# One decode step of attention beside an MLP: row 35 of w2 in other pieces, the MLP's bias loaded once, two rounds of V to an accumulator, the last V ahead of w2's row 14

## The chip, the core and the metric

One Trainium2 chip, of which the program uses one core. TensorE (PE, with PEld for its weight loads), VectorE (DVE), ScalarE (ACT), GpSimd (POOL) and SyncE (SP) run side by side; the core's 16 DMA engines bring the data from HBM. The metric is the device time of one execution in microseconds (us), as the median of several runs.

## What is computed

All arrays are float32. x is 2 x 576, the caches are 2 x 32 x 4096 x 128 (134 MB each), wq 576 x 4096, wo 4096 x 576, w1 576 x 4608, w2 4608 x 576.

```
x = A_x
g = sigmoid((x * gate_w).sum(-1))
q = x @ wq                         # 2 x 32 heads x 128
s = q . k_cache * 128**-0.5        # 2 x 32 x 4096
a = softmax(s) @ v_cache @ wo      # 2 x 576
h = gelu(x @ B_w1 + B_b1)          # 2 x 4608
b = h @ B_w2 + B_b2
out = g * a + (1 - g) * b
```

## The kernel before

**Memory.** One tile, `ring`, holds three slots of 64 KB in each of the 128 partitions. SP issues nearly all loads, in one fixed order: wq and w1, then K and V of 16 rounds (k0, v0, k1, v1, ...; each 8.39 MB, one slot, 64 KB to a partition), then three last pieces: rows 0 to 27 of w2; rows 28 to 35 of w2 with the first 16 rows of wo; the other 16 rows of wo. A load is issued when the slot that it goes to is free: after K of a round was reduced to scores (L518), or after TensorE has read V (L544). The transfers use eight completion semaphores in turn (DMAHW0 to DMAHW7 below), so a transfer also waits until the one eight before it has landed. ACT issues the small loads (x, the gate, the biases).

**A round (i = 0 to 15) is four heads of one batch entry.** DVE multiplies K by q in place (L508, `mul`) and sums over the 128 columns (L513, L514, `red`); POOL adds halves of a part of it first (L512). `max_p` (L518) takes each partition's largest score. `max_t` (L523) puts all partitions' maxima on each partition with a TensorE matmul, and `max_n` (L527) takes the maximum of each head, negated. ACT takes exp (L533, `softmax`) into the tile `p`. In the next round TensorE multiplies `p` with V (L544, `av`: 32 matmuls, each recorded as two, since float32 runs as two passes), DVE keeps the wanted diagonal blocks (L556, `keep`), and a matmul with `pick` adds them to the accumulator `oall` (L562, `combine`).

**Around the rounds.** Before them q (`proj` with wq) and the hidden layer of the MLP (`proj` with w1, then bias and gelu into `hg`) are made. After them come the products of `hg` with the rows of w2 (`mlp_out`, L369, into `acc`), the normalisation of `oall` (`norm_sum`, `norm_t`, `o_turn`), and the products with the rows of wo: rows 0 to FOLD - 1 into `acc` (`wo_out`, L369), the others into `res` (`last_out`, L459), to which `acc`, copied by ACT (L448), is folded (L469). The order of TensorE's work there is written out by hand.

**Row 35 of w2.** "Row r" is, for each partition p, the r-th of the 36 rows of w2 that p holds; row 35 is thus 128 places of 576 numbers. In the kernel before, the first 288 columns of it come with rows 28 to 34, in place; the other 288 columns come in four transfers, each over four partitions with eight places each (`wx`, L155), and are multiplied in `mlp_x` with a copy of `hg` spread to the same 16 partitions (`hx`).

Of the kernel before, what the change touches and what calls it, by code (L numbers as in the profile page):

```python
# [19 lines left out]
def kernel(  # L20
# [50 lines left out]
    FOLD = 23  # L71
# [11 lines left out]
    qp = ctx.enter_context(tc.tile_pool(name="qp", bufs=2))  # L83
# [51 lines left out]
    XE, XC = 4, 4  # L135
    XP = XE * XC
    XS = P // XP
    srcx2 = w2.rearrange("(e c s r) n -> c r e s n", e=XE, c=XC, s=XS)[:, NF - 1, :, :, DS:]

    def length(w, a, z):  # L140
        return XS * DS if w == "wx" else (z - a) * D - (DS if (w, z) == ("w2", NF) else 0)

    def load_last(m):
# [5 lines left out]
        for w, a, z in LAST[m]:  # L149
            if w == "wx":  # L150
                xt = t[:XP, o:o + XS * DS]
                rows[w] = xt.rearrange("p (s n) -> p s n", s=XS)
                o += XS * DS
                for c in range(XC):
                    nc.sync.dma_start(xt[c::XC].rearrange("e (s n) -> e s n", s=XS), srcx2[c])  # L155
                continue
            if (w, z) == ("w2", NF):
                nc.sync.dma_start(t[:, o:o + length(w, a, z)], srcs[w][:, a * D:z * D - DS])
                for r in range(a, z):
                    rows[w, r] = t[:, o + (r - a) * D:o + min((r - a + 1) * D, length(w, a, z))]  # L160
                o += length(w, a, z)
# [53 lines left out]
    def load_b1(b, ends):  # L215
        to, src = b1r.rearrange("(g q) n -> g q n", g=NG)[:, b], b1.rearrange("(g n) -> g n", g=NG)
        for u, v in zip(ends, ends[1:]):
            nc.scalar.dma_start(to[:, u:v], src[:, u:v])  # L218


    load_b1(0, (0, F4))
# [11 lines left out]
    idsc = cp.tile([P, P], F32, name="idsc")  # L233
    nc.scalar.mul(idsc, ident, SCALE)

# [6 lines left out]
    for j in range(NPB):  # L242
        t = cp.tile([P, NT * EB + 32 - EB], F32, name=f"p{j}")
# [6 lines left out]
    sel = ident.rearrange("p (j c) -> p j c", j=4)[:, :, :EB].rearrange("p j (e r) -> p j e r", e=E)  # L250
    selr = cp.tile([P, RB], F32, name="selr")
    nc.vector.tensor_reduce(selr, sel.rearrange("p j e r -> p r j e"), AX.XY, ALU.add)
    pick = cp.tile([P, 2 * NO - E], F32, name="pick")
    nc.vector.memset(pick, 0.0)
    nc.vector.tensor_reduce(pick[:, NO - E:NO], sel.rearrange("p j e r -> p e j r"), AX.XY, ALU.add)
# [61 lines left out]
    load_b1(1, (0, 232, 464, 696, 928, F4))  # L317
# [14 lines left out]
    nc.scalar.copy(qall, qps2)  # L332
# [65 lines left out]
    hb = ht[:, :, :B]  # L398
# [13 lines left out]
    for s in range(XS):  # L412
        nc.tensor.matmul(
            hxps[:, s], ident.rearrange("p (q s) -> p s q", s=XS)[:, s], hg[:, NF - 1], start=True, stop=True
# [4 lines left out]
    def mlp_x():  # L419
        for s in range(XS):  # L420
            acc_mm(hx[:, s], rows["wx"][:, s], s, lo=1)

    def mlp_out(lo, hi):
        for r in range(lo, hi):
            acc_mm(hg[:, r], rows["w2", r], r)
# [19 lines left out]
    def last_out():  # L445
# [18 lines left out]
        for r in range(FOLD, 31):  # L464
            for s in range(NC):
                part(r, s)
            if r == FOLD + 3:
# [53 lines left out]
    def max_t(i):  # L521
        mt[i] = ps_sm.tile([P, P], F32, tag="sm", name=f"mt{i}")
        nc.tensor.matmul(mt[i], mx[i].to_broadcast([P, P]), idsc, start=True, stop=True)  # L523

    def max_n(i):
        bias[i] = sp.tile([P, E], F32, tag="bs", name=f"bs{i}")
        nc.vector.tensor_reduce(bias[i], mt[i].rearrange("o (e p) -> o e p", e=E), AX.X, ALU.max, negate=True)  # L527

    def softmax(i):
        p = pt[i % NPB][:, :NT * EB].rearrange("p (t c) -> p t c", c=EB)  # L530
        for e in range(E):
# [3 lines left out]
                bias=bias[i][w, e:e + 1], scale=SCALE, accum_out=rs[w, i * E + e:i * E + e + 1],  # L535
# [3 lines left out]
    def av(i):  # L539
        ps = ps_av.tile([P, 512], F32, tag="av", name=f"av{i}")  # L540
        p = pt[i % NPB]
        for t in range(NT):
# [3 lines left out]
                p[:, EB * t:EB * t + 32],  # L546
                vt[i][:, RB * t:RB * (t + 1)].rearrange("p r d -> p (r d)"),
                start=(t < 4),
                stop=(t >= NT - 4),
            )  # L550
        avs[i] = ps
# [9 lines left out]
    def combine(i):  # L561
        nc.tensor.matmul(  # L562
            oall, pick[:, NO - E - i * E:2 * NO - E - i * E], avs[i].rearrange("p r d -> p (r d)"),
            start=(i == 0), stop=(i == N - 1), skip_group_check=True,
# [19 lines left out]
    for i in range(N):  # L584
        k = i - 1
        if 0 <= k:
            max_n(k)
# [12 lines left out]
        if 0 <= k:  # L600
            keep(k)
# [51 lines left out]
```

## Time and the profile before

| | before |
|---|---|
| time, median of 3 runs (lowest to highest) | 721.52 us (721.48 to 721.54) |
| span of the profiled execution | 719.8 us |
| DMA queue of SP, share of 16 engines' time in that span | 99.2% |
| read from HBM | 308.59 MB |
| busy: DVE, PE, POOL, ACT | 516.8, 237.2, 143.8, 38.3 us |
| PE instructions recorded | 1695 matmuls and as many weight loads |

The span runs from the first to the last instruction of one profiled execution. Its own run's time is not listed; the median is 1.7 us above the span, which is what lies around it. A busy share is an average over stages with different limits, so it is read stage by stage.

### The profile page before, as it was taken

What the parts mean: (1) busy time and instruction counts of PE and PEld (TensorE: products, weight loads), DVE (VectorE), ACT (ScalarE), POOL (GpSimd) and SP (SyncE); (2) the same over time, 40 slices, a digit from 0 to 9 for tenths busy, and PEclk for the clock granted to TensorE, in tenths of its full rate; (3) what the DMA queues carried; (4) which work ended last, traced back from release to release, by engine and by line L of the source; (5) the groups of instructions that cost most, each with busy time, mean ns of one, the idle gap of its engine ahead of it and who ended that gap; (6) DMA issues with size and microseconds to landing.
All of it is one profiled execution on the core that took longest, in us unless ns stands there. A gap on an engine that the chain in (4) does not pass through costs nothing.

```text
span 719.8 us, 3981 instructions
## 1 busy us (share of the span) xinstructions
PE 237.2 (33%) x1695; PEld 72.1 (10%) x1695; DVE 516.8 (72%) x146; ACT 38.3 (5%) x143; POOL 143.8 (20%) x31
## 2 busy tenths in 40 slices
PE   0682022230516060504142140506060503224198
PEld 0330000010101010101010010101010101001033
DVE  0104969789695969596969879696969596978900
ACT  0010010100001010101010100101010101010000
POOL 1000130404050403022040404040503113040400
PEclk9986557575757565755757575757575665757589
DMA  9999999999999999999999999999999999999997
GB/s 409 412 443 431 433 441 419 455 416 448 426 444 427 426 438 430 437 430 441 434 433 433 437 427 437 426 437 434 441 430 444 427 437 422 433 441 431 418 425 307
DMA packets 7277, 308.84 MB, mean 429 GB/s; under 512 B 830, under 2 KB 1362, under 8 KB 1628
## 3 DMA queue, kind: packets, MB, share of 16 engines
q1 hardware_dynamic: 7204, 308.55, 99.2%
q8 instruction: 13, 0.21, 0.1%
q10 hardware_dynamic: 56, 0.05, 0.0%
q14 instruction: 4, 0.03, 0.0%
HBM read 308.59 MB, written 0.00 MB: 429 GB/s over the span
## 4 chain that ended last, share of the span: by engine, by line
DMA 46%; DVE 35%; PE 16%; issue 1%; ACT 1%; ACTq 0%; POOL 0%; DVEq 0%; SPq 0%; POOLq 0%
DMA ring<-in_A_k_cache_dram 41%; DVE ring L508 19%; DVE s L513 10%; PE av L544 8%; DVE s L514 5%; DMA ring<-in_A_wo_dram 3%; DMA ring<-in_gate_w_dram 3%; PE hps L305 2%; PE qps L305 2%; PE oall L562 1%; PE acc L369 1%; PE mt L523 1%; ACT p L533 1%; ACTq L218 0%; DVE m L518 0%
## 5 line engine op out<-in xcount | busy, mean ns | idle before, releaser
L508 DVE TENSOR_TENSOR ring<-ring,q 128x16384 f32<-128x16384 f32 x16 | 275.6, 17225 | 108.9 <-DMA ring<-in_A_k_cache_dram 108.9
L512 POOL TENSOR_TENSOR ring<-ring 128x3968 f32<-128x3968 f32 x16 | 137.0, 8564 | 494.3 <-DVE ring L508 494.3
L513 DVE TENSOR_REDUCE s<-ring 128x66 f32<-128x8448 f32 x16 | 143.2, 8953 | 1.3
L544 PE MATMUL av<-ring,p 128*32 128x512 f32 x1024 | 133.7, 681 | 11.5 <-ACT p L533 6.2
L523 PE MATMUL mt<-idsc,m 128*128 128x128 f32 x32 | 12.6, 498 | 367.5 <-DVE m L518 367.5
L514 DVE TENSOR_REDUCE s<-ring 128x62 f32<-128x3968 f32 x16 | 68.4, 4276 | 0.0
L533 ACT ACTIVATE p<-s,bs 32x128 f32<-32x128 f32 x64 | 25.5, 398 | 487.8 <-DVE bs L527 486.6
L544 PEld LDWEIGHTS av<-ring,p 128*32 128x32 f32 x1024 | 35.6, 124 | 119.3 <-issue 102.4
L523 PEld LDWEIGHTS mt<-idsc,m 128*128 128x128 f32 x32 | 8.0, 310 | 383.2 <-DVE m L518 289.1
L353 PE MATMUL qb<-qm,spread 64*128 64x512 f32 x8 | 8.3, 1138 | 71.2 <-POOL qm L349 71.2
L562 PE MATMUL oall<-avs,pick 128*64 128x512 f32 x32 | 30.6, 1059 | 0.8 <-DVE avs L556 0.8
L556 DVE TENSOR_TENSOR avs<-av,selr 128x512 f32<-128x512 f32 x16 | 10.9, 680 | 16.1 <-PE av L544 16.1
L392 DVE TENSOR_TENSOR ring<-hps,ring 128x384 f32<-128x384 f32 x3 | 1.7, 558 | 27.2 <-PE hps L305 27.0
L263 DVE COPY ring<-ring 3x64 f32<-3x64 f32 x2 | 0.3, 180 | 19.8 <-DMA ring<-in_gate_w_dram 19.8
L349 POOL TENSOR_TENSOR qm<-qall,mine 64x512 f32<-64x512 f32 x4 | 4.1, 1032 | 38.4 <-ACT qall L332 38.4
L533 ACT ACTIVATION_READ_ACCUMULATOR p<-s,bs 32x1 f32 x64 | 11.8, 184 | 0.0
L369 PE MATMUL acc<-ring,hg 128*2 128x288 f32 x142 | 11.6, 456 | 0.0
L305 PE MATMUL hps<-ring 128*32 128x384 f32 x120 | 11.5, 549 | 0.0
L305 PE MATMUL qps<-ring 128*32 128x512 f32 x80 | 11.4, 737 | 0.0
L353 PEld LDWEIGHTS qb<-qm,spread 64*128 64x128 f32 x8 | 2.0, 307 | 74.2 <-POOL qm L349 74.2
L479 DVE COPY ring<-res 2x144 f32<-2x144 f32 x1 | 0.3, 298 | 12.6 <-PE res L483 12.6
L272 PE MATMUL xps<-ident,ring 3*128 3x3 f32 x10 | 1.3, 250 | 23.1 <-DMA ring<-in_gate_w_dram 23.1
(89 smaller groups left out, 75.3 us busy)
## 6 DMA issues: line engine op xcount, KB each, us to landing
ring<-in_B_w_dram SPq DMA_DIRECT2D x2, 4608.0 KB, 34.4
ring<-in_B_w_dram SPq DMA_DIRECT2D x2, 4032.0 KB
ring<-in_A_wo_dram SPq DMA_DIRECT2D x2, 2304.0 KB, 15.0
ring<-in_B_w_dram SPq DMA_DIRECT2D x1, 2160.0 KB
ring<-in_A_wo_dram SPq DMA_DIRECT2D x1, 2016.0 KB
ring<-in_B_w_dram SPq DMA_DIRECT2D x1, 1152.0 KB, 14.7
ring<-in_A_wo_dram SPq DMA_DIRECT2D x1, 1152.0 KB
ring<-in_A_wq_dram SPq DMA_DIRECT2D x1, 1024.0 KB
```

What stands on the lines that cost most here:

```text
L305: nc.tensor.matmul(ps[32 * j:32 * j + 32, :width], lhs, ts[c][:, o:o + width], start=(k == 0), stop=last, skip_group_check=True,)
L353: nc.tensor.matmul(ps, spread, t.rearrange("p u d -> p (u d)"), start=True, stop=True)
L369: nc.tensor.matmul(acc[o:o + m], lhsT, rhs[:, (s - lo) * DS:(s - lo + 1) * DS], start=start, stop=stop, skip_group_check=True)
L508: nc.vector.tensor_mul(kt[i], kt[i], qs[i].unsqueeze(1).to_broadcast([P, R, DH]))
L512: nc.gpsimd.tensor_add(t[:, :, :DH2], t[:, :, :DH2], t[:, :, DH2:])
L513: nc.vector.tensor_reduce(st[i][:, HALVED:], kt[i][:, HALVED:], AX.X, ALU.add)
L514: nc.vector.tensor_reduce(st[i][:, :HALVED], t[:, :, :DH2], AX.X, ALU.add)
L523: nc.tensor.matmul(mt[i], mx[i].to_broadcast([P, P]), idsc, start=True, stop=True)
L533: nc.scalar.activation(p[w, :, e * RB:(e + 1) * RB], st[i][w].rearrange("p (t c) -> p t c", c=RB), AF.Exp, bias=bias[i][w, e:e + 1], scale ...
L544: nc.tensor.matmul(ps[32 * j:32 * j + 32], p[:, EB * t:EB * t + 32], vt[i][:, RB * t:RB * (t + 1)].rearrange("p r d -> p (r d)"), start=(t ...
L556: nc.vector.tensor_mul(t, avs[i].rearrange("p (r d) -> p r d", d=DH), selr.unsqueeze(2).to_broadcast([P, RB, DH]))
L562: nc.tensor.matmul(oall, pick[:, NO - E - i * E:2 * NO - E - i * E], avs[i].rearrange("p r d -> p (r d)"), start=(i == 0), stop=(i == N - ...
```

## The change

It does these things:

- **Row 35 of w2.** Partitions 0 to 31 get their place of row 35, all 576 columns, in place, by a transfer of its own. The other 96 places come in four transfers, each over six partitions with four places each.
- **Bias of the MLP.** b1 was added to each batch row before the transpose, and so was loaded twice (one transfer, and five small ones later). Now it is loaded once, into a third row, and added after the transpose by one more DVE operation.
- **Maximum.** The TensorE matmul L523 and its scaled identity `idsc` are gone: DVE transposes blocks of 32 x 32 instead. The factor 128**-0.5 is applied to q rather than in exp.
- **Accumulating V.** Two rounds go to one accumulator, the one to its upper, the other to its lower half; `keep` and `combine` are done once for two rounds.
- **End.** TensorE's last product with V stands behind row 13 of w2, no longer behind row 23; the rest of w2 is in other places; FOLD is 27 instead of 23.
- TensorE's program has 140 instructions fewer. The q tile has one buffer instead of two.

```diff
-    FOLD = 23
+    FOLD = 27
-    qp = ctx.enter_context(tc.tile_pool(name="qp", bufs=2))
+    qp = ctx.enter_context(tc.tile_pool(name="qp", bufs=1))
...
-    XE, XC = 4, 4
+    XE, XC, XS = 6, 4, 4
     XP = XE * XC
-    XS = P // XP
-    srcx2 = w2.rearrange("(e c s r) n -> c r e s n", e=XE, c=XC, s=XS)[:, NF - 1, :, :, DS:]
+    XD = P - XP * XS
+    srcx2 = w2.rearrange("(p r) n -> p r n", r=NF)[XD:, NF - 1].rearrange("(e c s) n -> c e s n", e=XE, c=XC)
...
             if (w, z) == ("w2", NF):
-                nc.sync.dma_start(t[:, o:o + length(w, a, z)], srcs[w][:, a * D:z * D - DS])
+                n = (z - 1 - a) * D
+                nc.sync.dma_start(t[:, o:o + n], srcs[w][:, a * D:(z - 1) * D])
+                nc.sync.dma_start(t[:XD, o + n:o + n + D], srcs[w][:XD, (z - 1) * D:])
...
-    load_b1(0, (0, F4))
+    nc.scalar.dma_start(b1r.rearrange("(g q) n -> g q n", g=NG)[:, B], b1.rearrange("(g n) -> g n", g=NG))
...
-    idsc = cp.tile([P, P], F32, name="idsc")
-    nc.scalar.mul(idsc, ident, SCALE)
...
-    load_b1(1, (0, 232, 464, 696, 928, F4))
...
-    nc.scalar.copy(qall, qps2)
+    nc.scalar.mul(qall, qps2, SCALE)
...
-    hb = ht[:, :, :B]
+    hb = temp(NF * B).rearrange("p (r b) -> p r b", b=B)
+    nc.vector.tensor_add(hb, ht[:, :, :B], ht[:, :, B:B + 1].to_broadcast([P, NF, B]))
...
     def max_t(i):
-        mt[i] = ps_sm.tile([P, P], F32, tag="sm", name=f"mt{i}")
-        nc.tensor.matmul(mt[i], mx[i].to_broadcast([P, P]), idsc, start=True, stop=True)
+        mt[i] = sp.tile([P, PE_], F32, tag="mt", name=f"mt{i}")
+        nc.vector.transpose(mt[i], mx[i].to_broadcast([P, PE_]))
...
     def av(i):
-        ps = ps_av.tile([P, 512], F32, tag="av", name=f"av{i}")
+        half = i % 2
+        if half == 0:
+            avs[i // 2] = ps_av.tile([P, 512], F32, tag="av", name=f"av{i // 2}")
+        ps = avs[i // 2]
...
-    mlp_out(0, 24)
+    mlp_out(0, 14)
     av(k)
     load_next(("v", k))
     assert not seq
-    keep(k)
-    combine(k)
+    keep(k // 2)
+    mlp_out(14, 18)
+    combine(k // 2)
...
     norm_sum()
-    mlp_out(24, 30)
+    mlp_out(18, 28)
     norm_t()
-    mlp_out(30, 33)
+    mlp_x()
     o_turn(turn)
-    mlp_out(33, NF)
-    mlp_x()
+    mlp_out(28, NF)
     wo_out(0, FOLD)
     last_out()
```

**TensorE, from the products with V of rounds 13 and 14 to the end.** `acc<-ring,hg` is a row of w2 (two matmuls a row), `acc<-ring,hx` the wx part of row 35, `acc<-ring,oP` a row of wo. Before:

```order
L544 MATMUL av_1121<-ring,p_114 32x512 x32
L523 MATMUL mt_1165<-idsc,m_1163 128x128
L562 MATMUL oall<-avs_1167,pick 64x512
L369 MATMUL acc<-ring,hg 2x288 x48
L544 MATMUL av_1224<-ring,p_114 32x512 x32
L562 MATMUL oall<-avs_1264,pick 64x512
...
L369 MATMUL acc<-ring,oP 2x288 x46
L459 MATMUL res<-ring,oP 2x144 x16
L469 MATMUL res<-ring,fold 2x144 x4
L459 MATMUL res<-ring,oP 2x144 x18
```

And of the change:

```order
L558 MATMUL oall<-avs_1071,pick 64x512
L541 MATMUL av_1083<-ring,p_112 32x512 x32
L362 MATMUL acc<-ring,hg 2x288 x28
L541 MATMUL av_1083<-ring,p_112 32x512 x32
L362 MATMUL acc<-ring,hg 2x288 x8
L558 MATMUL oall<-avs_1203,pick 64x512
...
L362 MATMUL acc<-ring,oP 2x288 x54
L453 MATMUL res<-ring,oP 2x144 x4
L463 MATMUL res<-ring,fold 2x144 x4
L453 MATMUL res<-ring,oP 2x144 x14
```

Behind the product with V of round 14 nothing stands any more that waits for DVE's maximum of round 15; the last product with V moved ahead of 20 matmuls of w2, and four rows of wo moved from `res` to `acc`.

**SP, from rows 28 on of w2 to the third piece of wo, with what each waits for.** Before:

```order
L158 DMA ring<-in_B_w_dram 128x4320 [waits DMAHW5_49,DVE_49]
L155 DMA ring<-in_B_w_dram 4x8x288 [waits DMAHW6_49]
L155 DMA ring<-in_B_w_dram 4x8x288 x3
L166 DMA ring<-in_A_wo_dram 128x4608
L166 DMA ring<-in_A_wo_dram 128x4608 [waits DMAHW7_49]
L166 DMA ring<-in_A_wo_dram 128x4032 [waits DMAHW0_49,PE_49]
```

And of the change:

```order
L159 DMA ring<-in_B_w_dram 128x4032 [waits DMAHW0_49,DVE_49]
L160 DMA ring<-in_B_w_dram 32x576
L155 DMA ring<-in_B_w_dram 6x4x576 x3
L155 DMA ring<-in_B_w_dram 6x4x576 [waits DMAHW1_49]
L168 DMA ring<-in_A_wo_dram 128x4608 [waits DMAHW2_49]
L168 DMA ring<-in_A_wo_dram 128x4608 [waits DMAHW3_49]
```

There is one transfer more, so each transfer of wo now waits for the landing of the transfer one further on than before: the second one for rows 14 to 27 of w2.

## Rows read from the trace of the kernel before

**Rows 1.** The page: DMA queues; packets, MB, share of 16 engines.

```profile
q1 hardware_dynamic: 7204, 308.55, 99.2%
q8 instruction: 13, 0.21, 0.1%
```

**Rows 2.** Windows of three stretches; busy by engine, PEclk, DMA share, GB/s.

```profile
40.00:60.00 20.00, 14.87 (x133) 4.64 (x130) 3.55 (x4) 0.84 (x2) 1.03 (x1) 0.82 1.02 440
60.00:680.00 620.00, 171.96 (x1040) 47.15 (x1040) 503.54 (x102) 31.65 (x125) 139.99 (x19) 0.62 1.00 433
680.00:711.00 31.00, 28.34 (x297) 9.68 (x301) 5.48 (x14) 1.96 (x8) 0.00 (x0) 0.88 0.99 424
```

**Rows 3.** Windows of the last transfers, in the same columns.

```profile
713.00:715.00 2.00, 1.59 (x42) 0.96 (x40) 0.00 (x0) 0.40 (x1) 0.00 (x0) 1.00 0.81 315
715.00:717.00 2.00, 1.59 (x42) 0.94 (x44) 0.00 (x0) 0.00 (x0) 0.00 (x0) 1.00 0.33 105
...
715.00:715.50 0.50, 0.22 (x8) 0.20 (x12) 0.00 (x0) 0.00 (x0) 0.00 (x0) 1.00 0.57 198
716.00:716.50 0.50, 0.45 (x16) 0.13 (x8) 0.00 (x0) 0.00 (x0) 0.00 (x0) 1.00 0.24 74
```

**Rows 4.** The chain that ended last: its start and duration in us, what.

```profile
696.96 19.57 DMA ring<-in_A_wo_dram
...
716.57 0.41 PE res L459 x4
```

**Rows 5.** DVE's multiplication by lines, and the K and V loads' time to landing.

```profile
L508 DVE TENSOR_TENSOR ring<-ring,q 128x16384 f32<-128x16384 f32 x16 | 275.6, 17225 | 108.9 <-DMA ring<-in_A_k_cache_dram 108.9
...
DMA to landing us min/median/max: 27.4/27.5/27.6
```

**Rows 6.** Groups by lines: busy us, mean ns | idle before.

```profile
L523 PE MATMUL mt<-idsc,m 128*128 128x128 f32 x32 | 12.6, 498 | 367.5 <-DVE m L518 367.5
...
L556 DVE TENSOR_TENSOR avs<-av,selr 128x512 f32<-128x512 f32 x16 | 10.9, 680 | 16.1 <-PE av L544 16.1
...
L527 DVE TENSOR_REDUCE bs<-mt 128x4 f32<-128x128 f32 x16 | 4.6, 290 | 5.4 <-PE mt L523 5.4
...
L435 DVE STREAM_TRANSPOSE ring<-oT 128x32 f32<-128x32 f32 x2 | 0.3, 192 | 0.0
```

**Rows 7.** ACT's timeline at the start: start, us, what.

```profile
3.83 1.28 ACT L234 ACT_TABLE_LOAD   x1 [3.83 <-POOL ring L322]
...
38.66 2.68 ACTq L218 DMA_DIRECT2D ring<-in_B_b_dram  x5
```

**Rows 8.** SP's timeline: rows 28 to 35 of w2, and all of wo.

```profile
681.50 0.33 SPq L158 DMA_DIRECT2D ring<-in_B_w_dram  x1
...
685.15 15.32 SPq L166 DMA_DIRECT2D ring<-in_A_wo_dram  x9
```

**Rows 9.** TensorE's timeline at the end; in brackets its idle time before, and releaser.

```profile
684.47 7.67 PE L369 MATMUL acc<-ring,hg 128*2 128x288 f32 x96
...
686.35 0.15 PEld L369 LDWEIGHTS acc<-ring,hg 128*2 128x2 f32 x4 [0.33 <-issue]
...
691.96 7.05 PE L544 MATMUL av<-ring,p 128*32 128x512 f32 x64
...
707.18 5.43 PEld L369 LDWEIGHTS acc<-ring,oP 128*2 128x2 f32 x92 [0.49 <-issue]
...
713.17 0.84 PEld L459 LDWEIGHTS res<-ring,oP 128*2 128x2 f32 x32 [0.56 <-DMA ring<-in_A_wo_dram]
...
715.28 0.84 PEld L459 LDWEIGHTS res<-ring,oP 128*2 128x2 f32 x32 [1.02 <-DMA ring<-in_A_wo_dram]
```

**Rows 10.** Windows in which TensorE stops after a product with V.

```profile
650.00:660.00 10.00, 5.36 (x52) 1.51 (x44) 9.00 (x1) 0.00 (x0) 0.00 (x0) 1.00 0.99 428
660.00:670.00 10.00, 0.00 (x0) 0.00 (x0) 9.90 (x2) 0.00 (x0) 1.54 (x1) 0.51 0.96 415
```

**Rows 11.** DMA queues from 714 to 715.5 us, around one instruction packet.

```profile
q8 instruction: 1, 0.02, 4.0%
```

More of the change, by code (lines that the diff above doesn't have):

```diff
@@ L157, in load_last @@
             if (w, z) == ("w2", NF):
-                nc.sync.dma_start(t[:, o:o + length(w, a, z)], srcs[w][:, a * D:z * D - DS])
+                n = (z - 1 - a) * D
+                nc.sync.dma_start(t[:, o:o + n], srcs[w][:, a * D:(z - 1) * D])
+                nc.sync.dma_start(t[:XD, o + n:o + n + D], srcs[w][:XD, (z - 1) * D:])
                 for r in range(a, z):
-                    rows[w, r] = t[:, o + (r - a) * D:o + min((r - a + 1) * D, length(w, a, z))]
-                o += length(w, a, z)
+                    rows[w, r] = t[:XD if r == NF - 1 else P, o + (r - a) * D:o + (r - a + 1) * D]
+                o += n + D
                 continue
@@ L213 @@
     load()
[L215 to L218, printed above, removed]
-    load_b1(0, (0, F4))
+    nc.scalar.dma_start(b1r.rearrange("(g q) n -> g q n", g=NG)[:, B], b1.rearrange("(g n) -> g n", g=NG))
     for b in range(B):
@@ L413 @@
         nc.tensor.matmul(
-            hxps[:, s], ident.rearrange("p (q s) -> p s q", s=XS)[:, s], hg[:, NF - 1], start=True, stop=True
+            hxps[:, s], ident[:, XD:].rearrange("p (q s) -> p s q", s=XS)[:, s], hg[:, NF - 1], start=True, stop=True
         )
@@ L420, in mlp_x @@
         for s in range(XS):
-            acc_mm(hx[:, s], rows["wx"][:, s], s, lo=1)
+            acc_mm(hx[:, s], rows["wx"][:, s], s)
     def mlp_out(lo, hi):
         for r in range(lo, hi):
-            acc_mm(hg[:, r], rows["w2", r], r)
+            acc_mm(hg[:XD if r == NF - 1 else P, r], rows["w2", r], r)
     KB = DH // 32
@@ L466, in last_out @@
                 part(r, s)
-            if r == FOLD + 3:
+            if r == FOLD:
                 for s in range(NC):
@@ L545, in av @@
                 ps[32 * j:32 * j + 32],
-                p[:, EB * t:EB * t + 32],
+                p[:, 32 * t + EB * (1 - half):32 * t + EB * (1 - half) + 32],
                 vt[i][:, RB * t:RB * (t + 1)].rearrange("p r d -> p (r d)"),
-                start=(t < 4),
-                stop=(t >= NT - 4),
+                start=(half == 0 and t < 4),
+                stop=(half == 1 and t >= NT - 4),
             )
-        avs[i] = ps
     def keep(i):
@@ L562, in combine @@
         nc.tensor.matmul(
-            oall, pick[:, NO - E - i * E:2 * NO - E - i * E], avs[i].rearrange("p r d -> p (r d)"),
-            start=(i == 0), stop=(i == N - 1), skip_group_check=True,
+            oall, pick[:, NO - G - i * G:2 * NO - G - i * G], avs[i].rearrange("p r d -> p (r d)"),
+            start=(i == 0), stop=(i == N // 2 - 1), skip_group_check=True,
         )
@@ L599 @@
         max_t(i)
-        if 0 <= k:
-            keep(k)
-            combine(k)
+        max_n(i)
+        if 0 <= k and k % 2:
+            keep(k // 2)
+            combine(k // 2)
     k = N - 1
-    max_n(k)
     softmax(k)
-    mlp_out(0, 24)
+    mlp_out(0, 14)
     av(k)
@@ L610 @@
     assert not seq
-    keep(k)
-    combine(k)
+    keep(k // 2)
+    mlp_out(14, 18)
+    combine(k // 2)
     turn = late(P)
```

24 lines of the change are left out of this document (12 added, 12 removed).

## The prediction

> **What bounds the kernel now.** I read the table of DMA queues first. SP's queue carries 308.55 MB, and its packets fill 99.2% of the time of 16 engines [rows 1]. The windows show where: a share of 1.02 while w1 gives way to the first K, 1.00 in the 620 us of the rounds, 0.99 from 680 to 711 [rows 2]. An engine that is always busy can't be fed faster, so only fewer bytes, a better spread of the last bytes over the 16 engines, or a shorter tail behind them can shorten the run; a load issued too late can lengthen it. The rate is 433 GB/s, so 27.1 GB/s on each engine.
>
> DVE looks busy (517 us), and the chain of waits runs through it; but it waits 108.9 us for K in 16 rounds, 6.8 us in each [rows 5]. So it is not the bound: whatever it saves is added to that wait.
>
> The end is read in the windows from 713 on: the DMA share falls to 0.81, then to 0.33 [rows 3]. The engines stop one after another. The work left is 2 x 0.81 + 2 x 0.33 = 2.28 us of all 16, so an even spread would end at 715.28; but the share is still 0.24 between 716.0 and 716.5, and the chain has the last landing at 716.53 [rows 4]. The latest engine thus ends 1.2 us behind the mean. After it TensorE needs the last rows of wo, then two copies and the output follow: 719.8 - 716.5 = 3.3 us, whose code does not change.
>
> **The change, part by part.**
>
> *Row 35.* Before, each of 16 engines moved 8 x 1,152 = 9,216 bytes of it in place (0.34 us at 27.1 GB/s), and the four transfers put 147,456 bytes on the engines that serve four partitions; on four engines that is 36,864 bytes, 1.36 us each. Now the place of 32 partitions is 2 x 2,304 = 4,608 bytes an engine (0.17 us), and 221,184 bytes on six engines are again 36,864 each, 1.36 us. So an engine without such a transfer before and after ends 0.17 us sooner; one with them before and after too; one that is new to them ends 1.36 - 0.17 = 1.19 us later. That four partitions use four engines and six use six is no row's; bounds come from the shapes: one engine would take 221,184 bytes, 8.2 us; sixteen 0.51 us. I take six, since the largest number that could share six partitions' pieces evenly without cutting one is six.
>
> The Trainium skill, DMA: Bandwidth & Descriptors, Rules for kernel authors, speaks against such a shape: a transfer whose outermost dimension is under 16 is confined to that many engines, and all 16 should be used. By it the 96 places cost 1.36 us instead of 0.51, 0.85 more, if the others stood idle meanwhile. The rows of this case have no such idleness: those four transfers were issued between 681.5 and 685.2, with wo's behind them [rows 8], and the share stayed at 0.99 [rows 2], so the trace does not bear that price out here. By the rows the sum is -0.17, by the rule +0.85 on top of it.
>
> Is the latest engine one that gains? In 715.0 to 715.5 the share is 0.57 [rows 3], so about seven of 16 have stopped by 715.25. One of these, given 1.19 us more, ends by 716.4, about where the latest ends now. So the term is **-0.17 us** if the new engines are early ones; else at worst +1.19. In the other direction the most that a better spread can give is -1.2.
>
> *The bias.* Five transfers of together 18 KB over four partitions go: 4.6 KB on an engine, 0.17 us. They sit on the engines of the old wx transfers if those are the same four; 0 for the latest engine otherwise. I take 0 (bound -0.17). The 2.68 us that ACT spent issuing them [rows 7] lie before round 0, beside a full queue.
>
> *Fewer instructions.* The queue of instructions brings 13 packets, 0.21 MB [rows 1]; over 2 x 1,695 records that is 63 bytes each, so 140 fewer are 8.8 KB, about half a packet. One packet takes 4.0% of 16 x 1.5 us, 0.96 us of one engine [rows 11]. So one packet goes, or none: 0 to -0.96 us on one engine, and nothing for the next latest. I take 0.
>
> *The rounds.* TensorE loses L523 (32 records) and half of L562; DVE loses the 5.4 us of waiting for L523 and eight of 16 L556 at 680 ns, and gets 16 transposes; a 128x32 one took 192 ns in L435 [rows 6]. Its maximum then reads 32 numbers instead of 128, at most the 290 ns of L527. So from the maximum to exp a round gets shorter. What it feeds is the next load's issue, and a V load lands 27.4 to 27.6 us after its issue [rows 5], of which its own 8.39 MB take 19.4: up to 8 us of queue stand before it, and earlier issues only lengthen that. 0 us. One buffer for q makes ACT's copy wait until DVE's multiplication of that round ended; DVE needs the copy only after its two sums, over 13 us later. 0.
>
> *Before the rounds.* ACT's table load (1.28 us, first in its queue [rows 7]) now stands in front of the gate's exp, and one DVE addition is new. Behind them wait DVE's copies for q; they lie beside w1's transfer (share 1.02). 0, and with that cover gone 1.5 us.
>
> *SP's queue.* One more transfer at the end costs an issue of about 0.4 us between 681.5 and 685.2, and wo's transfers wait for landings one place later. The second piece of wo now waits for rows 14 to 27 of w2. In front of it then lie rows 28 to 35 with wx and wo's first piece, about 4.7 MB, 11 us of queue. Cover enough: 0; without it the whole delay would count.
>
> *TensorE's end.* Its work on w2 and V starts sooner: nothing waits for the maximum of round 15 ahead of w2's row 0, and the last product with V (691.96 to 699.0 [rows 9]) needs only exp, so it can stand some 6 us earlier. What V frees is the slot of wo's third piece, issued sooner into a queue that is not empty: 0. Four rows of wo move to `acc`, 16 records at 5.43/92 = 0.059 us, 0.94 us; before them TensorE waited for data at 713.17, and behind them it waited 1.02 us until 715.28 [rows 9]. So they fit into that wait, and the copy of `acc` just so. The fold moves behind it: eight records of 0.84/32 = 0.026, 0.2 us, in front of waits for later rows. I take 0; bounds 0 and +0.5 (below).
>
> **Sum.** -0.17 against the profiled span of 719.8 us; the median lies 1.72 above that span, so 721.52 - 0.17 = 721.35, about **721.4 us**. A measurement of this kernel can hardly tell less than 0.2%, 1.4 us, from no change; this is a tenth of that.
>
> **The rivals.**
>
> *A new engine is a late one.* About nine of 16 engines stop after 715.25 [rows 3]. If one of the newly loaded ends near 716.3 without the new load, it ends near 717.4, and the run gets 0.9 to 1.2 us longer: about 722.5. For it: no row names the engine of a packet. Against it: the four with extra pieces are likely among the late ones, so that most of the other late places are taken by engines that instruction packets held up [rows 11], and an engine that neither held up has room for 1.19 us. The same skill page (Why a DMA increments its semaphore by 16 and not by 1) has a transfer of SP take the lowest-numbered engines; by it the six are the old four and two more, always the same. No row here shows it. Chance 0.12.
>
> *TensorE becomes the last.* With its work 6 us earlier it stops and waits for each piece of wo. After the product with V of round 14 the granted clock fell from 1.00 to 0.51 with no work [rows 10]; at the lower of the two levels (1.2 instead of 2.4 GHz) a record takes about twice as long: at 686.35, soon after a long wait, (0.15 + 0.33)/4 = 0.12 us instead of 0.059 [rows 9]. Then the 16 records from 713.2 on take 1.9 us, the copy and the fold end near 715.9, and rows 28 to 31 run beyond the last landing: +0.5 us, 721.9; if the piece before is late too, +1. It decides if the clock is low at 713. The skill's page TensorE: Matmul & The Clock Gate, Why this matters for your kernels, warns of gaps between bursts; the trace agrees in the row just named, but the gaps here are shorter. Chance 0.12.
>
> *Loads come too late: slower.* Should DVE's maximum of a round come more than 8 us later than now, a V load would start late, each us beyond counting in every round: 15 us for one us. Nothing in the order of DVE's work adds more than 0.5 us a round, while it idles 6.8. Chance 0.04: 723 and more.
>
> *A clear gain.* It needs over 1.4 us, but an even end gives only 1.2 and 0.17 fewer bytes on the latest. Chance 0.03: below 720.1.
>
> **How the numbers follow.** The forecast keeps 0.69. It spans 721.0 (another engine's packet gone, some spread gained) to 721.6. With TensorE last the range reaches 722.0; the new late engine and both outer cases stay mostly outside, 0.19. So 720.9 to 722.0. Faster by over 0.2% takes 0.03, slower 0.04 plus a little of the second rival's worst, 0.05; the rest, 0.92, is no change.
>
> **What would show it.** The share of the DMA from 60 to 711 stays at 0.99 to 1.00, and the last landing lies at 716.2 to 716.5. If a new engine is late, the share is over 0 beyond 716.6. If TensorE is last, L453 no longer waits for wo before its last rows, and the clock of 713 to 715 is below 1.00. Loads too late show as a DMA share under 0.98 in the rounds. The prediction is wrong if the six partitions fall on fewer engines, or if an edit thought hidden stops the queue.

## The result and the profile after

| | before | changed |
|---|---|---|
| time, median (lowest to highest) of 5 runs each | 721.52 us (721.40 to 721.59) | 724.07 us (722.62 to 724.84) |
| ratio, 95% interval | | 1.0032 (1.0021 to 1.0042) |
| span of the profiled execution | 719.8 us | 720.7 us |
| the same execution's time | not listed | 722.62 us |

The change makes the kernel slower: by 0.32% by the ratio, and by 2.55 us between the two medians. That lies outside the range that was predicted. Two things are to be kept apart. The profiled execution is the fastest of the five, so its trace shows only 0.9 us of the loss. And the times of the changed kernel spread over 2.2 us, where those of before lie within 0.2.

The windows of the changed kernel, in the columns of [rows 2]: the rounds, then the last transfers.

```profile
60.00:680.00 620.00, 152.42 (x992) 37.69 (x996) 499.81 (x105) 31.29 (x124) 140.00 (x19) 0.61 1.00 433
...
691.00:697.00 6.00, 6.00 (x73) 2.05 (x68) 2.02 (x6) 0.00 (x0) 0.00 (x0) 1.00 1.00 390
697.00:711.00 14.00, 10.96 (x131) 3.63 (x127) 0.76 (x4) 0.00 (x0) 0.00 (x0) 0.88 1.00 427
...
713.00:715.00 2.00, 1.16 (x17) 0.32 (x16) 0.00 (x0) 0.16 (x1) 0.00 (x0) 1.00 0.88 351
715.00:717.00 2.00, 1.32 (x43) 1.16 (x46) 0.00 (x0) 0.24 (x1) 0.00 (x0) 1.00 0.40 137
```

The same window of the kernel before:

```profile
691.00:697.00 6.00, 6.00 (x68) 2.00 (x64) 0.00 (x0) 0.00 (x0) 0.00 (x0) 1.00 1.01 424
```

The rounds are as before: 1.00 and 433 GB/s [rows 2]. From 691 to 697, while row 35 is moved, the engines are as busy as before and move 390 GB/s instead of 424: their packets take longer. That is 34 x 6 / 433 = 0.47 us of the whole queue, and the shares of 713 to 717 (0.88 and 0.40 against 0.81 and 0.33 [rows 3]) show it still there: 2 x (0.07 + 0.07) = 0.28 us of all 16 engines.

The last packet of wo ends at 716.81 in this trace and at 716.50 in that of before, 0.31 us later.

The end of the chain of waits, after [rows 4]; TensorE's timeline, in the columns of [rows 9]; and SP's timeline:

```profile
696.07 19.56 DMA ring<-in_A_wo_dram
715.63 0.04 issue
715.68 0.43 PE res L453 x8
716.11 0.24 PE res L463 x8
716.35 0.84 PE res L453 x26
```

```profile
701.91 2.12 PE L362 MATMUL acc<-ring,oP 128*2 128x288 f32 x32
...
706.12 3.81 PE L362 MATMUL acc<-ring,oP 128*2 128x288 f32 x32 [2.09 <-DMA ring<-in_A_wo_dram]
...
715.68 0.43 PE L453 MATMUL res<-ring,oP 128*2 128x144 f32 x8 [0.90 <-DMA ring<-in_A_wo_dram]
```

```profile
718.04 0.28 SPq L483 DMA_DIRECT2D out_dram<-ring  x1
```

From row 27 of wo on (715.68) TensorE no longer waits for data: row 27, the fold and rows 28 to 31 follow each other, and the output is issued at 718.04, 0.33 us later than before (717.71). Earlier, TensorE did wait: 2.09 us before 706.12, and 32 records then took 3.81 us, at a mean granted clock of 0.66 from 706 to 711, where the 32 ahead of them, for rows 0 to 7, took 2.12.

Behind the output there is more. SP's waits at the end, before and after (us in total, times, longest):

```profile
SPq L648 <- DMA out_dram<-ring: 0.7, 1, 0.7
SPq L648 <- PEq L648: 0.6, 2, 0.4
```

```profile
SPq L643 <- DMA out_dram<-ring: 1.0, 1, 1.0
SPq L643 <- PEq L643: 0.9, 2, 0.7
```

Both waits are 0.3 us longer: 0.33 + 0.3 + 0.3 makes the 0.9 us of span. The table of DMA queues from 716.9 us to behind the span's end (packets, MB, share) has three packets of code, one of q8 and two of q14 (q14 carries 8 KB packets of code; its two lie behind the span's end):

```profile
q8 instruction: 1, 0.02, 0.9%
q14 instruction: 2, 0.02, 0.6%
```

Before has none of them there, but one more packet of q14 within its span, near 634 us (4 in the span; changed 3).

### The profile page after: what moved, and what is told of

Same layout as the page of the kernel before. It is cut to its first block, busy times and chain, and to the rows that moved or that the text cites. A ratio compares the mean times of both kernels' runs of the same rounds, so it can differ in the third digit from the quotient of the medians.

```text
span 720.7 us, 3828 instructions
## 1 busy us (share of the span) xinstructions
PE 214.4 (30%) x1625; PEld 61.5 (9%) x1625; DVE 514.1 (71%) x155; ACT 37.9 (5%) x142; POOL 144.2 (20%) x31
## 4 chain that ended last, share of the span: by engine, by line
DMA 48%; DVE 35%; PE 15%; issue 1%; ACT 0%; ACTq 0%; SPq 0%; DVEq 0%; POOL 0%; POOLq 0%
DMA ring<-in_A_k_cache_dram 39%; DVE ring L502 19%; DVE s L507 10%; PE av L541 10%; DVE s L508 5%; DMA ring<-in_B_w_dram 4%; DMA ring<-in_gate_w_dram 3%; DMA ring<-in_A_wo_dram 3%; PE oall L558 2%; PE qps L299 1%; PE acc L362 1%; DVE avs L552 1%; ACT p L527 0%; DVE m L512 0%; PE zps L275 0%
## 5 line engine op out<-in xcount | busy, mean ns | idle before, releaser
L541 PE MATMUL av<-ring,p 128*32 128x512 f32 x1024 | 139.2, 705 | 173.9 <-ACT p L527 173.9
L558 PE MATMUL oall<-avs,pick 128*64 128x512 f32 x16 | 14.9, 1029 | 197.8 <-DVE avs L552 168.9
L362 PE MATMUL acc<-ring,hg 128*2 128x288 f32 (+1 forms) x144 | 12.9, 501 | 25.5 <-DMA ring<-in_B_w_dram 25.5
L558 PEld LDWEIGHTS oall<-avs,pick 128*64 128x64 f32 x16 | 2.2, 196 | 204.6 <-DVE avs L552 204.6
L552 DVE TENSOR_TENSOR avs<-av,selr 128x512 f32<-128x512 f32 x8 | 5.5, 682 | 11.0 <-PE av L541 11.0
L362 PE MATMUL acc<-ring,oP 128*2 128x288 f32 x108 | 9.2, 479 | 3.7 <-DMA ring<-in_A_wo_dram 3.7
```

The source lines that it names most:

```text
L362: nc.tensor.matmul(acc[o:o + m], lhsT, rhs[:, (s - lo) * DS:(s - lo + 1) * DS], start=start, stop=stop, skip_group_check=True)
L541: nc.tensor.matmul(ps[32 * j:32 * j + 32], p[:, 32 * t + EB * (1 - half):32 * t + EB * (1 - half) + 32], vt[i][:, RB * t:RB * (t + 1)].rea ...
L552: nc.vector.tensor_mul(t, avs[i].rearrange("p (r d) -> p r d", d=DH), selr.unsqueeze(2).to_broadcast([P, RB, DH]))
L558: nc.tensor.matmul(oall, pick[:, NO - G - i * G:2 * NO - G - i * G], avs[i].rearrange("p r d -> p (r d)"), start=(i == 0), stop=(i == N // ...
```

## The experiments

The letters A, B, C, R, S, P and W name theories, each explained in the expectation that first uses it. Each experiment ran beside the kernel before on its chip (medians of before 721.57 to 721.64, within 721.38 to 721.96). "Late" is a time clearly above the lowest group of the same kernel. The intervals of single ratios are some 0.0009 to each side, 0.65 us, so steps of 0.1 to 0.3 us between medians count only where a trace shows the same. The median of a kernel whose times lie in groups moves with the mix of the groups: that of the changed kernel is 724.07, 723.15 and 724.01 in three series.

### Is it row 35, TensorE's clock, or the end?

**e1: the changed kernel again.** 

> The changed kernel as it is, for a second profile and five more times. Three theories. A (clock): TensorE is done with w2 some 5 us earlier, waits for the pieces of wo between 700 and 715, and the granted clock falls to the lower level there; where the low stretch falls on the last rows of wo, TensorE ends up to 1.5 us later, and where it falls earlier, as in the profile at hand (0.66 in 706 to 711, 1.00 from 711 on), nearly nothing is lost. A expects times spread over 722.6 to 724.8 again, and in a profile with a span over 721.5 a granted clock under 0.8 somewhere between 711 and 717.5. B (row 35): the six partitions' transfers end late on some DMA engines; B expects the DMA share over 0.1 beyond 716.8 in a profile with a longer span, at a clock of 1.00. C (code at the end): the fold behind row 27 and the waits behind the output cost a constant 0.8 us; C expects no spread of its own.

723.15 us (722.78 to 724.60), 1.0027 (1.0016 to 1.0037). The profile fell on the lowest time: 405 GB/s from 691 to 697, clock 1.00 to the end.

**e2: row 35 as before** (the diff's parts on `wx`, `load_last` and `hxps` undone). 

> The changed kernel with row 35 split as before (right half over four partitions' transfers, left half in place). A: no change beside the changed kernel, about 724, spread over 2 us. B: back to 721.5 to 722.3. C: as the changed kernel.

722.62 us (722.44 to 723.21), 1.0015 (1.0006 to 1.0024). The late times are gone and a constant 1.0 us stays: B holds for the spread, something else for the rest. Its rate from 691 to 697 is 428 GB/s.

**e3: TensorE's wait put back.**

```diff
     softmax(k)
+    hold = ps_sm.tile([1, 1], F32, tag="sm", name="hold")
+    nc.tensor.matmul(hold, bias[k], ones, start=True, stop=True)
     mlp_out(0, 14)
```

> The changed kernel with one more TensorE instruction ahead of row 0 of w2, which waits for DVE's maximum of round 15, as TensorE did before. A: TensorE starts w2 near 684.5 instead of 679.8, works without a pause until about 711, the clock is 1.00 to the end, and the time is 721.9 to 722.6 with a spread under 0.6 us. B and C: no change beside the changed kernel, about 724.

724.00 us (722.72 to 724.41), 1.0028 (1.0017 to 1.0038): no help. But the edit did not do what it was to do; TensorE still waited for wo:

```profile
710.76 1.62 PE L362 MATMUL acc<-ring,oP 128*2 128x288 f32 x12 [2.65 <-DMA ring<-in_A_wo_dram]
```

**e4: the kernel before with the new row 35 alone** (the same parts of the diff applied). 

> The kernel before with the split of row 35 alone (96 places over six partitions, 32 in place). A and C: 721.2 to 721.9, a spread of 0.3 us. B: 722.5 to 724.

722.88 us (721.67 to 724.31), 1.0015 (1.0006 to 1.0024), in three groups: five times of 721.67 to 722.01, four of 722.88 to 723.21, two of 724.3. Row 35 alone makes late times. The profile is one of the last group. Its windows, the DMA queue from 717 to 718.3 us, and TensorE's timeline:

```profile
691.00:697.00 6.00, 6.00 (x72) 2.02 (x64) 0.00 (x0) 0.00 (x0) 0.00 (x0) 1.00 1.02 404
...
717.00:718.50 1.50, 1.45 (x28) 0.90 (x32) 0.00 (x0) 0.00 (x0) 0.00 (x0) 0.50 0.05 15
```

```profile
q1 hardware_dynamic: 30, 0.02, 5.3%
```

```profile
713.50 1.17 PE L461 MATMUL res<-ring,oP 128*2 128x144 f32 x32 [0.61 <-DMA ring<-in_A_wo_dram]
...
717.05 2.33 PE L461 MATMUL res<-ring,oP 128*2 128x144 f32 x34 [2.13 <-DMA ring<-in_A_wo_dram]
```

From 717 on 5.3% of 16 x 1.3 us, 1.1 us, are left: one engine, over 1 us behind the last landing of before. TensorE waits 2.13 us for it; by then the granted clock has fallen to 0.50, so that 34 records take 2.33 us, where 32 took 1.17 at 713.50. So the lower clock does cost time, some 1.1 us, but behind a late engine. The packet records show what made it late: from 716.70 to 718.05 its packets follow each other without a pause, and each takes as long as elsewhere (2,304 bytes in 93 ns). It had more to do.

### Row 35: how many engines, or where it is written?

**e7: 48 places over six partitions, 80 in place**, on the kernel before: `XE, XC, XS = 6, 2, 4`. 

> The kernel before with 48 places of row 35 over six partitions (two transfers) and 80 in place. Theory R: an engine that moves both a share of the six partitions' pieces and one more instruction packet than others ends last; its share is now 18,432 + 11,520 bytes, 1.11 us, instead of 1.53 with 96 places and 0.34 for an engine without a share before. R expects the later times nearer: groups at about 721.7, and late ones at 722.4 to 723.2 in place of 722.9 to 723.2 and 724.3. A rival, that the one issue more on SP or the other order of its waits makes the late times, expects the groups of the 96 places again.

723.30 us (723.08 to 724.13), 1.0025 (1.0015 to 1.0035). Fewer places on the six, and yet every run is late: theory R alone falls.

**e8: 64 places over four partitions, 64 in place**: `XE, XC, XS = 4, 4, 4`. 

> The kernel before with 64 places of row 35, whole rows, over four partitions (four transfers) and 64 in place. The bytes on each engine are those of before (36,864 and 9,216), and the form, the number of transfers and the matmuls are those of the change. R: the four are the same engines as before, none of which carries instruction packets, so 721.4 to 721.9 with no late times. The rival (form, issue or waits of the new transfers): late times of 722.9 to 724.3 as with six.

722.37 us (722.16 to 722.70), 1.0011 (1.0003 to 1.0020): no late times, but 0.75 us that R did not expect. The window of 691 to 697 of e7 and then of e8 tells why:

```profile
691.00:697.00 6.00, 6.00 (x71) 1.91 (x62) 0.00 (x0) 0.00 (x0) 0.00 (x0) 1.00 1.03 334
```

```profile
691.00:697.00 6.00, 6.00 (x72) 1.89 (x68) 0.00 (x0) 0.00 (x0) 0.00 (x0) 1.00 1.04 389
```

Busy throughout, they move 334 and 389 GB/s: (424 - 334) x 6 / 433 = 1.25 us, and 0.48.

**e9: e7 with the 80 rows read from one contiguous block.**

```diff
-                nc.sync.dma_start(t[:XD, o + n:o + n + D], srcs[w][:XD, (z - 1) * D:])
+                nc.sync.dma_start(t[:XD, o + n:o + n + D], w2[:XD])
```

> As the experiment with 48 places over six partitions and 80 in place on the kernel before (723.3), but the 80 rows in place are read from the first 80 rows of w2, which lie behind each other in HBM, so that part of row 35 is not multiplied by its own weights. In that experiment the rate in 680 to 711 was 405 GB/s at a share of 1.00, where before has 424 at 0.99: the packets took longer. Theory S (place): it comes from where the rows are written, 80 partitions instead of 128; S expects 723.3 and 405 GB/s again. Theory H (source): it comes from reading rows that lie 82,944 bytes apart; H expects 420 GB/s or more and 722.0 to 722.6.

723.12 us (722.86 to 723.99), 1.0024 (1.0015 to 1.0033); 333 GB/s from 691 to 697. The source is not it.

**e10: e8 with the place written over all 128 partitions.**

```diff
-                nc.sync.dma_start(t[:XD, o + n:o + n + D], srcs[w][:XD, (z - 1) * D:])
+                nc.sync.dma_start(t[:, o + n:o + n + DS], srcs[w][:, (z - 1) * D:(z - 1) * D + DS])
```

> As the experiment with 64 places over four partitions and 64 in place on the kernel before (722.37, 415 GB/s in 680 to 711), but the transfer in place writes the left half of all 128 partitions instead of whole rows of 64: the same bytes on each engine, read at the same distance; the right half of 64 places of row 35 is left out, and the left half of the others is added twice. S: 128 partitions again, so 423 GB/s and 721.4 to 721.8. H, or the one transfer more: 722.4 again.

721.72 us (721.43 to 721.93), 1.0001 (0.9992 to 1.0010): as before, with 422 GB/s:

```profile
691.00:697.00 6.00, 6.00 (x68) 1.98 (x64) 0.00 (x0) 0.00 (x0) 0.00 (x0) 1.00 1.01 422
```

The bytes on each engine and the number of transfers are the same; part of row 35 is left out. The destination is wider, and so the rows written are shorter (1,152 bytes instead of 2,304). The row length alone is not it: the pieces over four partitions have rows of 2,304 bytes in both kernels, and in e10 these took 93 ns each, beside 422 GB/s. And the transfers beside a narrow destination are slowed too: the first packets of wo, 18,432 bytes each, took 689 ns on average from 690 to 700 us before and in e10, but 711 in the changed kernel, 733 in e8 and 782 in e7. Theory S is shown.

**e13: e4 in the same way**, a quarter of the columns of all 128 partitions in place of whole rows of 32. 

> The kernel before with 96 places of row 35 over six partitions, as in the change, but the transfer in place writes a quarter of the columns of all 128 partitions instead of whole rows of 32: the same bytes on each engine. Three quarters of 32 places of row 35 are left out, and a quarter of the others is added twice. Theory S alone (writes over fewer partitions slow the packets): the late times vanish, 721.3 to 721.8. Theory R (one of the two more engines also carries instruction packets): the rate in 680 to 711 is back at 424 GB/s, but a part of the times stays late, at 722.5 to 724.3. Both: fewer or smaller late times.

722.57 us (721.41 to 722.94), 1.0009 (1.0000 to 1.0018), at 435 GB/s: four times of 721.41 to 721.71, seven of 722.44 to 722.94, none of 724.

```profile
691.00:697.00 6.00, 6.00 (x72) 1.89 (x68) 0.00 (x0) 0.00 (x0) 0.00 (x0) 1.00 1.04 435
```

So both are at work: the narrow place, and, apart from it, the pieces over six partitions, which in part of the executions cost 1.0 us. With pieces over four (e10) this never happened. That six partitions mean two more engines with an extra share fits this, and no run shows it.

**e16: the changed kernel with that wide place.** 

> The changed kernel, but row 35's transfer in place writes a quarter of the columns of all 128 partitions instead of whole rows of 32 (the same bytes on each engine; three quarters of 32 places of row 35 are left out, a quarter of the others is added twice). Theory S: the rate in 691 to 697 is back at 424 GB/s or more (390 and 405 in the two profiles of the changed kernel), and the times over 723.7 vanish; with the two more engines still there, as in the experiment on before (721.4 to 722.9), the times are 722.4 to 723.8, the median 723.0. If the six engines alone made the late times, the median stays at 723.2 to 724.1 with times up to 724.8.

722.61 us (722.23 to 724.45), 1.0018 (1.0009 to 1.0027), 422 GB/s:

```profile
691.00:697.00 6.00, 6.00 (x72) 2.02 (x68) 2.06 (x6) 0.00 (x0) 0.00 (x0) 1.00 1.01 422
```

On the same chip:

**e18: the changed kernel a third time.** 

> The changed kernel once more, for a profile of another execution. S with a lasting part expects, if this execution is over 723.5, a rate under 410 GB/s in 697 to 711 as well; R alone expects 424 GB/s there and a share of 0.06 (one engine) beyond 717; A (clock) expects 424 GB/s, no data beyond 716.9 and a granted clock under 0.8 between 713 and 718.

724.01 us (722.94 to 724.60), 1.0033 (1.0022 to 1.0044). The narrow place alone is worth 1.4 us of the median there; one time of e16, 724.45, stays late, so it is not all. The 1.4 holds for these two series. On the kernel before, the same edit takes the median only from 722.88 (e4) to 722.57 (e13), and the pieces over six partitions are the larger part there: 0.9 from before to e13. The profile fell on the lowest time again (399 GB/s from 691 to 697, then 424), so that it tells nothing of late ones.

### The constant 1.0 us

**e5: eight more instructions on GpSimd**, on e2:

```diff
     nc.gpsimd.memset(rs, 0.0)
+    for _ in range(8):
+        nc.gpsimd.memset(rs, 0.0)
```

> The changed kernel with row 35 split as before (722.62), and eight more settings of a small tile to zero on GpSimd, early. In the traces of before and of the row-35 experiment on before, GpSimd's clearing of semaphores at the very end starts 0.02 us after the instruction ahead of it; in those of the changed kernel 0.34 us after it, and two packets of 8 KB follow behind the span, where before has one at 634 us. Theory P: GpSimd has some seven instructions fewer, so that its last piece of code is fetched only at the very end. P expects the packet of 8 KB back near 634 us, none behind the span, the clearing without a pause, and a time 0.5 to 0.7 us shorter: 721.9 to 722.1. Rival F: the constant 1.0 us lies in the fold behind row 27 and in the order of SP's last waits; F expects 722.6 again.

722.34 us (722.11 to 722.79), 1.0010 (1.0001 to 1.0019). SP's second wait at the end is back at its old length, and q14's packet back in the rounds:

```profile
SPq L643 <- DMA out_dram<-ring: 1.0, 1, 1.0
SPq L643 <- PEq L643: 0.6, 2, 0.4
```

That wait is 0.9 us in all seven profiles of kernels with the change's ends and without the eight instructions (changed, e1, e2, e3, e6, e16, e18), and 0.6 in all six with them (e5, e11, e12, e14, e15, e17). P is right in kind, and worth 0.3 us, not 0.5 to 0.7; that q14's packets are GpSimd's code is inferred from this. The granted clock was 0.50 from 711 to 713, and TensorE never waited behind 710.67.

**e6: the fold where it was**, on e2 (`FOLD = 23`, the fold at `r == FOLD + 3`). 

> The changed kernel with row 35 split as before (722.62), and with the fold where it stood before (rows 23 to 31 of wo into the result, the fold behind row 26). Theory F: the fold's eight records lie behind the landing of row 27, on the path; F expects 0.2 to 0.35 us less, 722.3 to 722.4, and the first copy of the result some 0.3 us sooner behind the last landing. Theory P alone: no change, 722.6. If the fold was hidden by the wait for row 31, no change either.

722.58 us (722.39 to 722.96), 1.0014 (1.0005 to 1.0023): nothing. Here too the clock was 0.50 from 711 to 713, and TensorE never waited behind 710.61. That it worked behind its data, so that the fold's place made no difference, is argued.

**e11: fillers in TensorE's gaps**, on e5: 40 matmuls, each begun afresh, all into one unused tile of two partitions. 

> As the experiment with row 35 as before and the eight more GpSimd instructions (722.34), with 40 more matmuls of wo's rows into an unused tile, in the gaps in which TensorE waits for pieces of wo: 18 behind row 7, 18 behind row 15, 4 behind row 22. Theory A (clock), which the wait put back did not decide since TensorE still waited for wo: the granted clock stays at 1.00 from 700 on, TensorE follows the last landing, and the time is 721.9 to 722.1. If A is wrong, 722.3 or, since the fillers stand in the queue, more.

735.51 us (735.08 to 735.76), 1.0193 (1.0179 to 1.0207). A miss of the edit: 18 such matmuls took 8.65 us, 0.24 us a record, and became the end.

```profile
703.99 8.65 PE L438 MATMUL idle<-ring,oP 128*2 128x288 f32 x35
```

**e14: the fillers spread over four groups of columns.**

```diff
+            for f in range(FILL.get(r, 0)):
+                o = 32 * (f % 4)
+                nc.tensor.matmul(
+                    idle[o:o + B], oP[:, :, r], rows["wo", r][:, :DS], start=f < 4, stop=False, skip_group_check=True
+                )
```

> As the fillers before, but 18, 18 and 5 of them, spread over four groups of columns so that they don't wait for each other (0.13 us each): they fill the gaps in which TensorE waits for rows 8 and 16 of wo. Base 722.34. Theory A (clock): 1.00 from 700 to the end, TensorE waits for the last landing and is done 0.3 to 0.5 us sooner: 721.9 to 722.1, and a smaller spread. If A is wrong: 722.3 or more at a clock of 1.00.

722.16 us (721.78 to 722.55), 1.0007 (0.9998 to 1.0016). Now 36 such records take 2.59 us, the clock stays at 1.00, and TensorE waits 0.75 us for row 27. The fillers in its timeline, and the windows:

```profile
708.22 2.59 PE L439 MATMUL idle<-ring,oP 128*2 128x288 f32 x36
...
715.67 0.43 PE L461 MATMUL res<-ring,oP 128*2 128x144 f32 x8 [0.75 <-DMA ring<-in_A_wo_dram]
```

```profile
711.00:713.00 2.00, 2.00 (x34) 0.80 (x28) 0.00 (x0) 0.00 (x0) 0.00 (x0) 1.00 0.99 412
713.00:715.00 2.00, 1.93 (x24) 0.72 (x18) 0.00 (x0) 0.02 (x1) 0.00 (x0) 1.00 0.85 332
```

The clock does what A expects. A gain in time is not shown: the 0.2 us between the medians lies inside the interval, and the output is issued at 718.04 in this profile (of an execution of 722.41 us) and at 718.06 in that of e5 (722.17).

**e17: e14 with the fold where it was.** 

> The changed kernel with row 35 as before, the eight GpSimd instructions, the 18, 18 and 5 spread fillers, and the fold behind row 26 as before: what is left of the change is the bias, the shorter rounds and the order of w2 and V. If the pieces add up, the fold takes 0.25 us off the 722.16 without it, since TensorE worked without a pause from row 27 on there: 721.8 to 722.0, at most 0.3 above before, which the order of SP's last waits can hold. If the fold was hidden, 722.1 to 722.3.

722.06 us (721.97 to 722.48), 1.0006 (0.9997 to 1.0015). The output is issued at 717.70, as before (717.71), and the span is 720.0:

```profile
717.70 0.29 SPq L491 DMA_DIRECT2D out_dram<-ring  x1
```

```profile
SPq L651 <- DMA out_dram<-ring: 1.0, 1, 1.0
SPq L651 <- PEq L651: 0.6, 2, 0.4
```

So some 0.4 to 0.5 us remain although the work ends as early as before: 0.2 to 0.3 in SP's first wait, and some 0.2 outside the span. Over the 11 executions the time lies 2.00 us above the span on average, over the 26 of before beside them 1.82. That average is 1.78 to 1.82 for the kernel before and the experiments on it, and 1.89 to 2.18 for the changed kernel and those on it, with or without the GpSimd instructions.

**e12: b1 in six pieces**, on e5, for as many transfers as before. 

> As the experiment with row 35 as before and the eight more GpSimd instructions (722.34), with the load of b1 cut into six pieces, so that the kernel has as many transfers as before. Theory W (waits): the semaphore of the output is the last that SP waits for at the end, as before, and not the first with four more waits of 0.06 us behind it; W expects 0.25 us less, 722.1. Rival: the order of these waits costs nothing that counts, 722.3, or the five issues and packets more cost 0.1 to 0.2.

722.63 us (722.05 to 723.48), 1.0015 (1.0006 to 1.0024). In the trace W holds: SP's first wait is 0.7 us again and the span 719.9. But that profile is of the fastest of the 11 executions. Over all of them the median span is 720.4, as in e5 (720.3), and the time lies 2.18 us above the span on average (e5: 2.03), so the times show nothing won. In this profile a packet of q14 again follows behind the span's end. Of the profiles whose own time is known, the 11 with such a packet have 1.92 to 2.15 us outside the span, the 8 without 1.77 to 1.94; that is a correlation, and no run shows its cause.

**e15: the changed kernel with e5's instructions and e14's fillers.** 

> The changed kernel, row 35 as changed, with the eight GpSimd instructions and the same fillers. If row 35 is what is left beside these two, the times lie 0.3 above the base of the fillers with row 35 as before and spread over 1 to 2 us: 722.2 to 723.5. If the lower clock was needed for the late times (a late engine lets TensorE idle and fall to half speed), the spread is under 0.7 us.

723.97 us (722.45 to 724.19), 1.0028 (1.0017 to 1.0039): with row 35 as changed, the two mends don't help. This profile is of a late execution (724.13):

```profile
691.00:697.00 6.00, 6.00 (x76) 2.04 (x68) 2.02 (x6) 0.00 (x0) 0.00 (x0) 1.00 1.03 398
697.00:711.00 14.00, 12.77 (x187) 5.02 (x185) 0.76 (x4) 0.00 (x0) 0.00 (x0) 1.00 0.99 383
711.00:713.00 2.00, 1.22 (x20) 0.34 (x18) 0.00 (x0) 0.00 (x0) 0.00 (x0) 1.00 0.99 378
```

Here the rate does not recover behind row 35: 383 and 378 GB/s, at a share of 0.99, where all other profiles are back at 419 to 427. From 697 to 711 that costs (424 - 383) x 14 / 433 = 1.3 us. The packets themselves are slow: those of 18,432 bytes of wo took 765 ns on average from 700 to 712 us, and 687 before.

## Why the prediction was wrong

**The step that failed first is "Row 35".** It priced the new place by its bytes, 4,608 on each engine at 27.1 GB/s, and found -0.17 us. The bytes are right; the rate is not. Behind it stands the premise that an engine that is always busy can't be fed faster: from 691 to 697 the share is 1.00, and yet 390 GB/s are moved instead of 424. While a transfer writes 32 partitions, the packets of all engines take longer, those of wo too. The runs show the size by the width of the destination: 0.48 us by the rate and 0.65 by the time at 64 partitions, none at 128 (e8, e10), and 1.25 by the rate at 80, with two transfers over six partitions besides (e7). They show that it is not the source (e9), and that without it the changed kernel's median falls by 1.4 us (e16, e18). The Trainium skill, DMA: Bandwidth & Descriptors, The descriptor swizzle, says that in a transfer to 128 partitions each engine writes through one port, its own; read so, a transfer to fewer partitions brings several engines to one port. The lower rate at each narrower width agrees with that; that 80 partitions cost more than 64 does not follow from it, and no run here shows a port.

**The rival "a new engine is a late one" came out in the times as well**, with its price about right: 0.9 to 1.2 us were worked out, and e13's two groups lie 1.0 apart. That the late engines are the new ones is not shown. Its chance of 0.12 looks too small: 7 of 11 executions there were late, and the trace of one execution could not have told it, since it changes from one to the next. That instruction packets on those engines make them late was argued, not shown. The Trainium skill's rule that was weighed (DMA: Bandwidth & Descriptors, Rules for kernel authors), to use all 16 engines, was set aside because the queue stayed full. It did stay full until the last transfers; in e4's late execution the idleness of the other engines is there at the end, where from 717 on one engine's work is left. Of the narrow place the rule does not speak. Of the signs that the prediction named, this profile of the fastest execution shows two weakly: the share is 0.07 from 716.5 to 717.0, and TensorE waits for no data behind 715.68, but the clock from 713 to 715 is 1.00.

**"Whose code does not change"** was said of the 3.3 us behind the last landing. The code there is also what ends the program: SP's waits and GpSimd's last instructions. Both became longer by 0.3 us in the trace. GpSimd's part, the second wait, is shown (e5, 0.3 us). The first wait is short again with as many transfers of b1 as before (e12's trace), but the times of e12 show no gain by it. The Trainium skill, Runtime: NRT & Kernel Launch, Instruction fetch mechanics, has the fetch of the next block as mostly hidden; e5 agrees for the rounds, and not at the program's end. What lies around the span grew too, by some 0.2 us (e17); a late fetch of code would agree with the packets of q14 behind the span's end, and is not shown.

**"Fewer instructions: 0"** held for DMA. **"The rounds: 0"**, **"SP's queue: 0"** and **"Before the rounds: 0"** held: share 1.00, 433 GB/s, and DVE's wait for K rose instead. "The bias: 0" was not tested by itself, since e12 changed more than it. DVE's multiplication in the lines of the changed kernel, after [rows 5]:

```profile
L502 DVE TENSOR_TENSOR ring<-ring,q 128x16384 f32<-128x16384 f32 x16 | 275.6, 17226 | 116.8 <-DMA ring<-in_A_k_cache_dram 116.8
```

**"TensorE's end: 0, bounds 0 and +0.5"**: the lower clock behind a wait for wo came as the rival said, mostly at 704 to 715, and where no engine is late it takes at most 0.2 us by the medians (e14), and 0.1 more with the fold (e17; e6 alone showed none). Neither is clear of the interval. The rival's +0.5 was not reached there; its +1, "if the piece before is late too", has 1.1 us beside it in the late execution of e4. The fold does not stand in front of waits for later rows, as the prediction had it: it stands behind the last wait.

**What adds up.** Of the 2.4 us on e18's chip: 1.4 from row 35 (e16; e2, with row 35 as before, leaves the same 722.6), 0.3 GpSimd's last code, 0.3 clock and fold (by medians only), and 0.4 to 0.5 in SP's first wait and around the span. What stays open: why 80 partitions cost more than 64, why the slow packets last to the end in some executions (one profile, e15), which engines are late and when, and what makes the 0.2 us around the span. No version here beats the kernel before; e10, which changes row 35 alone and leaves out part of it, equals it.

## What to carry to other kernels

Where the DMA is the bound, read its GB/s beside its share of busy time in the window of each transfer: a transfer to a part of the partitions can keep all engines busy at four fifths of the rate, and slow those beside it. It depends on the shape: beside transfers over four and six partitions the queue here kept 422 and 435 GB/s (e10, e13). A term worked out from bytes at the full rate is a lower bound until a row shows that shape at that rate. And when the instructions of an engine change in number, look at what follows the output: its last code and waits lie on the path, whatever they cost elsewhere.

## What was not expected of the hardware

- 80 of 128 partitions as destination: 334 GB/s from 691 to 697 at a share of 1.03 (e7), 64: 389, 32: 390 to 405, 128: 422 to 435. Pieces of wo move in that window too.
- Matmuls begun afresh into the same two partitions took 0.24 us a record (e11); four groups in turn, accumulating, 0.07 (e14). Two things differ between the two, and which one makes it is not shown.
- Times of one kernel can lie in groups 1 us apart (e13: 721.4 to 721.7 and 722.4 to 722.9) with the same instructions, and one profile shows one group.
